# Attention with q/k normalisation and a two-matmul feed-forward on one core: unit loads ahead of the weight loads, LN transposes on the DMA queue, q and k transposes on TensorE up to unit 7, later unit loads on GpSimd's queue

## The chip, the cores and the metric

The kernel runs on one core of one Trainium2 chip. The metric is the device time of one execution in microseconds (us). Engines in the views: PE is TensorE (PEld its weight loads), DVE is VectorE, ACT is ScalarE, POOL is GpSimd, SP is SyncE, which does nothing here but issue DMAs.

## The reference

```python
q_n, k_n = rmsnorm(q, g_q), rmsnorm(k, g_k)          # q, k, v: (8, 12, 448, 64) float32
scores = (1/8) * q_n @ k_n^T                         # per batch and head, 448 x 448
attn = softmax(scores); x = attn @ v                 # heads side by side: (8, 448, 768)
xn = layernorm(x) * g_ln                             # over 768
out = x + relu(xn @ w_ch1) @ w_ch2                   # w_ch1 768 x 3072, w_ch2 3072 x 768
```

## The kernel before, in words

The work is staged by batch. While PE does the feed-forward of batch b, the attention of batch b+1 is cut into small steps that are put between the feed-forward's chunks of six matmuls. Only the attention of batch 0 stands alone, ahead of everything.

**Units and pairs.** A *unit* is what is loaded and prepared in one go: from batch 1 on, four heads, that is two *pairs* of heads. Batch 0 has units 0 to 3 (one, one, two and two pairs), batch 1 has units 4, 5 and 6, batch 2 has units 7, 8 and 9, and so on to unit 24. `load_unit` fills one tile `qkv` with k, q and v by nine DMAs (a main one and two small "left" ones each); the pool has two such tiles, so unit u+2 is loaded when unit u has been read for the last time.

**Preparation of a unit** (`pieces`, called by one-letter names). `a`, `c`: squares of k and q on ACT (L196). `d`, `e`: their sums on DVE (L199). `g` (`gq`, `gk`): reciprocal roots on ACT (L56, L57). `i`: k times the product of the two gains, `kg`, on POOL (L205; on DVE for the units of `DVE_KG`). `j`, `k`: k as a high and a low half in float16 (`khi` on ACT or POOL, L213 or L211; `klo` on DVE, L216). `l`, `m`: scaled q and its second copy (L63, L256). `v`, `w` (`z` both): v cast to float16 on POOL (L262, L268).

**Transposes of q and k.** Below unit `DMA_UNIT` PE transposes each pair (`trans_k`, L290 and L293; `trans_q`, L304 and L307), seven matmuls each through the one PSUM tile `tr`, and DVE copies it out (L295, L312). From `DMA_UNIT` on, SP issues DMA transposes of a whole unit instead: `x` (k: one large, two small, L235 and L238) and `y` (q: three and two, L245 and L248).

**Attention of a pair.** Seven score blocks (`scores`, L326, L329, L330), each followed by ACT's exponential (`E`, L332), and seven blocks of `values` (L355, L357); then DVE divides and writes `x` (L370 to L377).

**LN and feed-forward.** `stats`, `A`, `N` (L499, L514, L519) give the normalised tile `xn`; `X` (`ln_trans`) transposes it on PE (L546) and copies it to `xnT` (L551, or L549 on ACT). A batch has three tiles of 128 tokens, an odd batch a fourth one (`xl`), made of the leftovers of two batches. `up` makes `hT` (PE L564, ACT L566) and `down` the result (PE L577, DVE L581).

**What sets the order.** PE, ACT, POOL and SP run in the order in which the program emits; DVE's order is by a scheduler after the first attention. The first attention follows the written table `ORDER`, whose words are the names above with a unit or pair (`a5`), `S`/`V` with pair and block, `L5` a unit load, `W0` to `W2` thirds of the first weight, `W3`, `W4` halves of the second. Weights are loaded from POOL's queue, since the DMA casts them to float16. After that, `attention` makes a list of steps, seven to a pair (step 7p + i), and gives each unit's pieces their steps; `run_rest` spreads the steps over a batch's chunks so that they end `tail` chunks before the batch does. At that point it emits the LN of the next batch (`ln_list`).

Of the kernel before, what the change touches and what calls it, by code (L numbers as in the profile page):

```python
# [28 lines left out]
DVE_KG, POOL_HI, POOL_DUP, ACT_Q = (0, 1), (1, 2, 3, 4), (1, 2, 4, 5), (0, 1)  # L29
# [42 lines left out]
class _Fast:  # L72


    def __init__(self, ctx, tc, sh, q, k, v, g_ln, w1, w2, out):
        self.g_ln = g_ln
# [26 lines left out]
        self.rr = fix.tile([128, 2, 7 * B * NPAIR], FP32, name="rr_all", tag="rr_all")  # L103
# [23 lines left out]
    def load_first(self):  # L127
# [44 lines left out]
    def pieces(self, u):  # L172
# [9 lines left out]
        def begin():  # L182
# [4 lines left out]
            c["rf"] = self.rr[:, :, o:o + g]  # L187
# [16 lines left out]
        def kg():  # L204
            (nc.vector if u in DVE_KG else nc.gpsimd).tensor_tensor(  # L205
                out=c["t"][1], in0=c["t"][1],
                in1=sh.gprod.unsqueeze(1).broadcast_to([128, g, D]), op=ALU.mult)
# [77 lines left out]
    def trans_k(self, p):  # L285
# [3 lines left out]
        kT, ps = self.kU[0][:, 960 * (p % 2):960 * (p % 2) + 960], self.tr  # L289
# [7 lines left out]
    def trans_q(self, p):  # L297
# [5 lines left out]
        qT = self.qU[0][:, p % 2].rearrange("p e s -> p (e s)")  # L303
# [9 lines left out]
        kT = self.kU[0][:, 960 * (p % 2):960 * (p % 2) + 960]  # L313
        self.prs[p] = dict(q=qT, main=kT[:, 192:960], left=kT[:, 0:192])

    def scores(self, p, i):
# [6 lines left out]
        ps = self.ps_s.tile([128, 512], FP32, tag="psS", name="psS")  # L323
# [4 lines left out]
        else:  # L328
# [4 lines left out]
                             scale=self.rr[:, 1, g:g + 1], bias=EXP_BIAS)  # L333
# [53 lines left out]
    def first_attention(self):  # L387
# [7 lines left out]
        for x in ORDER:  # L395
# [28 lines left out]
    def attention(self):  # L424
# [445 lines left out]
```

## Time and profile before

| | |
|---|---|
| median of 3 runs | 649.29 us (648.17 to 650.2) |
| profiled execution | 649.09 us, of which the span of the trace is 647.3 us |
| DVE, ACT, POOL busy | 293.0, 362.7, 103.1 us |
| DMA issues | 160 DMA transposes, 21 unit loads of nine DMAs each |
| HBM read, written | 52.36 MB, 11.01 MB |

Four stages follow one another in the span: batch 0's attention, up to 66.4 us; batch 0's feed-forward beside batch 1's attention, up to 150.07 us; six batches of the same kind, up to 577.96 us; and the feed-forward of batch 7 alone. In a row of a timeline the first number is the start, the second the duration, and brackets tell how long the engine was idle before it and what ended that. In a row of waits stand the total, the count and the longest.

### The profile page before, as it was taken

How to read it: one execution, taken by the hardware profiler on the slowest of the kernel's cores; microseconds unless marked ns; L12 is line 12 of the kernel's file. 1: busy time of each engine (PE TensorE's matmuls, PEld its weight loads, DVE VectorE, ACT ScalarE, POOL GpSimd, SP SyncE). 2: the span in 40 equal slices, each digit the busy share in tenths (PEclk: the TensorE clock that was granted, in tenths of full speed). 3: DMA queues.
4: the chain of work that ended last, by engine and by line, in shares of the span. 5: the costliest groups of instructions: out<-in, count | busy, mean ns of one | idle time of the engine just before them, and what ended most of it. 6: DMA issues, size and time to landing. Idle time of an engine off the chain costs nothing.

```text
span 647.3 us, 11504 instructions
## 1 busy us (share of the span) xinstructions
PE 594.3 (92%) x4506; PEld 349.6 (54%) x4506; DVE 293.0 (45%) x633; ACT 362.7 (56%) x673; POOL 103.1 (16%) x116
## 2 busy tenths in 40 slices
PE   2873957999999999999999999999999999999995
PEld 1552534565556666665556666665556666654563
DVE  5795504573425625672434625582443621380011
ACT  5974736644874368635874288626874277314300
POOL 2942310220210202220220111210221100000000
PEclk9996879899999999999999999999999999999998
DMA  8999985554255354564255355455243230010011
GB/s 231 246 220 221 200 178 120 140 140 157 62 141 131 94 130 119 110 151 113 55 133 139 90 132 119 113 140 126 66 107 79 71 62 4 25 50 0 2 50 53
DMA packets 149836, 73.12 MB, mean 113 GB/s; under 512 B 99728, under 2 KB 144784, under 8 KB 149776
## 3 DMA queue, kind: packets, MB, share of 16 engines
q1 hardware_dynamic: 140960, 62.82, 39.4%
q0 software_dynamic: 8528, 9.44, 8.6%
q8 instruction: 37, 0.61, 0.4%
q14 instruction: 23, 0.19, 0.1%
q10 hardware_dynamic: 288, 0.07, 0.0%
HBM read 52.36 MB, written 11.01 MB: 98 GB/s over the span
## 4 chain that ended last, share of the span: by engine, by line
PE 74%; DVE 8%; SPq 7%; DMA 4%; ACT 3%; issue 2%; POOL 0%; ACTq 0%; DVEq 0%; POOLq 0%
PE psH L564 32%; PE psC L577 25%; PE psS L326 7%; PE oA L355 4%; SPq L125 4%; DVE xn L519 3%; DMA qkv<-in_v_dram 2%; PE oB L357 1%; SPq L245 1%; SPq L117 1%; DVE stat L499 1%; PE psX L546 1%; DVE khl L216 1%; ACT E L332 1%; PE psS L329 1%
## 5 line engine op out<-in xcount | busy, mean ns | idle before, releaser
L564 PE MATMUL psH<-xnT,w 128*128 128x512 f16 (+1 forms) x1152 | 250.4, 358 | 0.0
L332 ACT ACTIVATE E<-psS,rr_all 128x448 f16<-128x448 f32 x336 | 207.8, 632 | 71.1 <-PE psS L326 64.6
L577 PE MATMUL psC<-w,hT 128*128 128x384 f16 x1344 | 241.8, 326 | 1.6 <-DVE x L581 1.6
L566 ACT ACTIVATE hT<-psH 128x384 f16<-128x384 f32 (+1 forms) x192 | 105.0, 547 | 132.0 <-PE psH L564 130.8
L577 PEld LDWEIGHTS <-hT 128*128 128x128 f16 x1344 | 124.1, 98 | 72.7 <-issue 2.2
L564 PEld LDWEIGHTS <-w 128*128 128x128 f16 x1152 | 106.0, 99 | 85.1 <-issue 4.7
L326 PE MATMUL psS<-qU,kU 128*128 128x448 f16 x288 | 104.3, 365 | 17.7 <-DMA qU<-qn 10.5
L355 PEld LDWEIGHTS <-E 128*128 128x128 f16 x1008 | 71.6, 99 | 63.9 <-ACT E L332 11.8
L205 POOL TENSOR_TENSOR qkv<-qkv,gprod 128x896 f32<-128x896 f32 x21 | 43.7, 2082 | 325.6 <-issue 253.0
L355 PE MATMUL oA<-v,E 128*128 128x65 f16 x864 | 68.0, 196 | 5.6 <-ACT E L332 5.2
L581 DVE SCALAR_TENSOR_TENSOR x<-psC,rs_all,x 128x384 f32<-128x384 f32 x48 | 29.5, 617 | 85.7 <-PE psC L577 85.1
L199 DVE TENSOR_REDUCE ssq<-khl 128x14 f32<-128x896 f32 (+1 forms) x25 | 26.2, 1048 | 80.1 <-ACT khl L196 80.0
L370 DVE RECIPROCAL rec_all<-oA 128x6 f32<-128x6 f32 x48 | 9.3, 194 | 98.3 <-PE oA L355 98.1
L357 PE MATMUL oB<-v,E 128*128 128x65 f16 x288 | 52.6, 195 | 0.1
L326 PEld LDWEIGHTS <-kU 128*128 128x128 f16 x288 | 28.6, 100 | 36.5 <-issue 17.4
L63 DVE SCALAR_TENSOR_TENSOR qn<-qkv,rr_all 128x256 f16<-128x256 f32 (+2 forms) x81 | 26.9, 393 | 19.9 <-ACT rr_all L57 19.9
L199 DVE TENSOR_REDUCE ssq<-qn 128x14 f32<-128x896 f32 (+1 forms) x25 | 26.1, 1045 | 20.4 <-ACT qn L196 20.4
L357 PEld LDWEIGHTS <-E 128*128 128x128 f16 x336 | 33.0, 98 | 0.6 <-DVE xl L377 0.4
L216 DVE TENSOR_TENSOR khl<-qkv,khl 128x896 f16<-128x896 f32 x21 | 22.8, 1088 | 10.9 <-ACT khl L213 10.9
L372 DVE TENSOR_TENSOR x<-oA,rec_all 128x384 f32<-128x384 f32 x48 | 26.8, 558 | 1.5
L499 DVE BATCH_NORM_STATS2 stat<-x 128x6 f32<-128x256 f32 x72 | 26.1, 415 | 0.7
L262 POOL CAST v<-qkv 128x768 f16<-128x768 f32 x21 | 17.4, 828 | 35.6 <-PE oB L357 19.6
(87 smaller groups left out, 356.9 us busy)
## 6 DMA issues: line engine op xcount, KB each, us to landing
qkv<-in_k_dram SPq DMA_DIRECT2D x21, 384.0 KB, 3.4
qkv<-in_q_dram SPq DMA_DIRECT2D x21, 384.0 KB, 3.9
qkv<-in_v_dram SPq DMA_DIRECT2D x21, 384.0 KB, 4.2
out_dram<-x SPq DMA_DIRECT2D x20, 384.0 KB, 2.5
w<-in_moe_w_ch_dram POOLq DMA_DIRECT2D x3, 1536.0 KB, 20.3
w<-in_moe_w_ch_dram POOLq DMA_DIRECT2D x2, 2304.0 KB, 45.2
qU<-qn SPq DMA_TRANSPOSE x100, 2.4
out_dram<-x SPq DMA_DIRECT2D x8, 192.0 KB, 2.3
```

The lines of the kernel that those rows point to most:

```text
L199: nc.vector.tensor_reduce(out=c["ssq"][:, n], in_=c["sq", n], axis=AX.X, op=ALU.add)
L205: (nc.vector if u in DVE_KG else nc.gpsimd).tensor_tensor(out=c["t"][1], in0=c["t"][1], in1=sh.gprod.unsqueeze(1).broadcast_to([128, g, D] ...
L216: nc.vector.tensor_tensor(out=c["khl"][:, :, 1], in0=c["t"][1], in1=c["khl"][:, :, 0], op=ALU.subtract)
L326: nc.tensor.matmul(ps[:, 0:S], c["main"][:, ts(i, 128)], q[:, ts(h, S)], start=True, stop=True)
L332: nc.scalar.activation(out=c["E"][:, i], in_=ps[:, 0:S], func=AFT.Exp, scale=self.rr[:, 1, g:g + 1], bias=EXP_BIAS)
L355: nc.tensor.matmul(oA[:, t, cs], E[:, i, ts(t, 128)], rhs, start=(i == 0 and t == 0), stop=(i == 6 and t == 2))
L357: nc.tensor.matmul(oB[:, cs], E[:, i, 320:448], rhs, start=(i == 0), stop=(i == 6))
L499: nc.vector.bn_stats(out=self.st[b][:, t, 6 * s:6 * s + 6], in_=x[:, 256 * s:256 * s + 256])
L564: nc.tensor.matmul(ps[:, 0:N], sh.w1[:, dc, ts(f, 128)], xnT[:, dc, 0:N], start=(dc == 0), stop=(dc == NDC - 1))
L566: nc.scalar.activation(out=hT[:, f, 0:N], in_=ps[:, 0:N], func=AFT.Relu)
L577: nc.tensor.matmul(ps[:, 0:384], hT[:, f, ts(t, 128)], sh.w2[:, f, ts(g, 384)], start=(f == 0), stop=(f == NFF - 1))
L581: nc.vector.scalar_tensor_tensor(out=x[:, ts(g, 384)], in0=ps[:, 0:384], scalar=self.rs[:, b, t:t + 1], in1=x[:, ts(g, 384)], op0=ALU.mult ...
```

## The change

- First loads: k of pair 0 and its leftovers go out from ACT's queue beside q's on SP; the two gains follow on SP. Their product is made by DVE in unit 0's `kg`, and `gmax` at `G2`.
- `ORDER` is another table. The loads of units 4 and 5 (`L4 L5`) stand right behind `G`; `W0` stands behind `i3` (unit 3's `kg`), `W1` and `W2` further on, `W3` behind `m4`; `W4` is emitted with unit 6's first pieces.
- Units 5 to 7 get their q and k transposed on PE (`DMA_UNIT` 8), units 5 and 6 prepared at given steps (`EARLY`). The DMA transposes remain from unit 8 on.
- Unit loads are emitted one step later than before; from unit 9 on they go out from POOL's queue instead of SP's.
- From batch 1 on `ln_trans` is one DMA transpose per tile on SP, with no PSUM tile and no copy; the LN stands in one piece, `tail` is 13 chunks instead of 10, and `xn` has four buffers.
- From pair 15 on every third score block uses `tr`'s bank.
- Unit 2's `kg` moves from POOL to DVE, unit 5's copy of q from POOL to DVE; the reciprocal roots of q and k are two exponentials instead of one.

```diff
-DVE_KG, POOL_HI, POOL_DUP, ACT_Q = (0, 1), (1, 2, 3, 4), (1, 2, 4, 5), (0, 1)
+DVE_KG, POOL_HI, POOL_DUP, ACT_Q = (0, 1, 2), (1, 2, 3, 4), (1, 2, 4), (0, 1)
 ORDER = """
-b0 c0 e0 a0 gq0 d0 b1 i0 G j0 z0 a1 k0 c1 l0 i1 gk0 m0 d1 K0 Q0 e1 b2 g1 a2 l1 j1 d2 m1 S0.0
...
+b0 c0 e0 a0 d0 b1 i0 gq0 a1 G L4 L5 j0 z0 k0 gk0 l0 i1 m0 d1 c1 K0 Q0 e1 b2 j1 g1 a2 S0.0 S0.1
...
-DMA_UNIT = 5
+DMA_UNIT = 8
+PE_SET = (DMA_UNIT + 1) % 2
+EARLY = {5: (42, 49), 6: (48, 57)}
...
-        for n in range(2):
+        for n, eng in ((0, nc.sync), (1, nc.scalar)):
+            main(eng, n, 0)
+            left(eng, n)
+        for n in range(2):
-            main(nc.sync, n, 0)
-            left(nc.sync, n)
+            nc.sync.dma_start(self.sh.gg[:, n], self.gs[n].unsqueeze(0).broadcast_to([128, D]))
...
     def load_unit(self, u):
+        eng = self.nc.sync if u < 9 else self.nc.gpsimd
         for n in (1, 0, 2):
-            self.load_main(self.nc.sync, n, t[:, n, 0:6 * m], b, hs, 2 * m)
-            self.load_left(self.nc.sync, n, t[:, n, 6 * m:7 * m], b, hs, 2 * m)
+            self.load_main(eng, n, t[:, n, 0:6 * m], b, hs, 2 * m)
+            self.load_left(eng, n, t[:, n, 6 * m:7 * m], b, hs, 2 * m)
...
         def root(n=slice(0, 2)):
-            _rsqrt(nc, c["rf"][:, n], c["ssq"][:, n], c["rt"][:, n], D * 1e-6)
+            nc.scalar.activation(c["rt"][:, n], c["ssq"][:, n], AFT.Ln, bias=D * 1e-6)
+            for i in range(2)[n] if isinstance(n, slice) else (n,):
+                nc.scalar.activation(c["r", i], c["rt"][:, i], AFT.Exp, scale=-0.5)
...
-        ps = self.ps_s.tile([128, 512], FP32, tag="psS", name="psS")
+        if p > UNIT_PAIR[DMA_UNIT] and (7 * p + i) % 3 == 2:
+            ps = self.ps_tr.tile([128, 512], FP32, tag="tr", name="psS3")
+        else:
+            ps = self.ps_s.tile([128, 512], FP32, tag="psS", name="psS")
...
             e = max(7 * (p - 2) - 1, st + 5)
+            st, e = EARLY.get(u, (st, e))
             pieces = ["bai", "d", "c", "e", "j", "gv", "k", "l", "m", "w", "x", "y"]
             k = len(pieces) - 2
+            if u < DMA_UNIT:
+                pieces = pieces[:k]
             if u < nu - 2 and f"L{u + 2}" not in done:
-                todo.setdefault(e, []).append(lambda u=u: self.load_unit(u + 2))
+                todo.setdefault(e + 1, []).append(lambda u=u: self.load_unit(u + 2))
...
+                if u == 6 and x == 0 and "W4" not in done:
+                    todo[at].append(lambda: self.load_w2(1))
...
-        return [call("A", "N0", "N1", "N2", "R")] + [
-            call(f"X{t}", *([f"N{t + 3}"] if t + 3 < n else [])) for t in range(n)]
+        return [call("A", "N0", "N1", "X0", "N2", "X1", *(["N3"] if n > 3 else []), "X2",
+                     *(["X3"] if n > 3 else []), "R")]
...
             self.xnT = self.p_m.tile([128, NDC, 512], FP16, tag="xnT", name="xnT")
+        if b:
+            nc.sync.dma_start_transpose(self.xnT[:, :, ts(t, 128)], xn)
+            return
...
-        tail = 10
+        tail = 13
```

Line numbers of the changed kernel lie some 6 to 27 above those of the kernel before. On POOL's queue during the first attention, the weights stood in the kernel before as follows (`w_76` is the first weight, in thirds of 1024 columns; `w_66` the second, in halves of 384, whose room v's first load uses until the casts `v` and `vl` have read it; `L205` on `hT` is unit 3's `kg`, on `qkv` unit 4's). Two thirds of the first weight had gone out six rows further up, ahead of unit 2's `kg`.

```order
L205 TENSOR_TENSOR hT<-hT,gprod 128x896
L262 CAST v_116<-w_66 128x12x64
L268 CAST vl<-w_66 64x2x64 x2
L473 DMA w_76<-in_moe_w_ch_dram 128x6x1024
L211 CAST khl<-hT 128x14x64
L478 DMA w_66<-in_moe_w_ch_dram 128x24x384 x2
L205 TENSOR_TENSOR qkv<-qkv,gprod 128x896
```

In the changed kernel the queue reads from unit 3's `kg` to unit 4's:

```order
L215 TENSOR_TENSOR hT<-hT,gprod 128x896
L497 DMA w_71<-in_moe_w_ch_dram 128x6x1024
L272 CAST v_111<-w_66 128x12x64
L278 CAST vl<-w_66 64x2x64 x2
L221 CAST khl<-hT 128x14x64
L497 DMA w_71<-in_moe_w_ch_dram 128x6x1024 x2
L215 TENSOR_TENSOR qkv<-qkv,gprod 128x896
```

and further on, from unit 4's last v casts:

```order
L278 CAST vl<-qkv 64x2x64 x2
L266 COPY qn<-qn 128x14x64
L502 DMA w_66<-in_moe_w_ch_dram 128x24x384
L215 TENSOR_TENSOR qkv<-qkv,gprod 128x896 x2
L502 DMA w_66<-in_moe_w_ch_dram 128x24x384
```

The first third of the first weight has moved from ahead of unit 2's `kg` to behind unit 3's, and the halves of the second weight from ahead of unit 4's `kg` to behind unit 4's last piece and behind the `kg` of units 5 and 6.

On SP's queue, the end of the stretch in which batch 1's attention runs reads as follows in the kernel before: one unit's load, another unit's k and q transposes, then batch 0's first stores.

```order
L117 DMA qkv<-in_k_dram 128x4x192
L125 DMA qkv<-in_k_dram 64x2x64 x2
L117 DMA qkv<-in_q_dram 128x4x192
L125 DMA qkv<-in_q_dram 64x2x64 x2
L117 DMA qkv<-in_v_dram 128x4x192
L125 DMA qkv<-in_v_dram 64x2x64 x2
L235 DMA_TRANSPOSE kU_112<-khl 128x12x128
L238 DMA_TRANSPOSE kU_112<-khl 128x2x64 x2
L245 DMA_TRANSPOSE qU_114<-qn 128x4x128 x3
L248 DMA_TRANSPOSE qU_114<-qn 128x2x64 x2
L605 DMA out_dram<-x 128x384
L605 DMA out_dram<-x 128x768 x2
```

In the changed kernel the same place has the k and q transposes of unit 8, the first that go by DMA, and the four LN transposes of batch 1:

```order
L245 DMA_TRANSPOSE kU_107<-khl 128x12x128
L248 DMA_TRANSPOSE kU_107<-khl 128x2x64 x2
L255 DMA_TRANSPOSE qU_109<-qn 128x4x128 x3
L258 DMA_TRANSPOSE qU_109<-qn 128x2x64 x2
L569 DMA_TRANSPOSE xnT<-xn 128x6x128 x4
L632 DMA out_dram<-x 128x384
L632 DMA out_dram<-x 128x768 x2
```

The unit load has gone from the queue, and `xnT` stands between the unit's transposes and the stores.

The load now stands on POOL's queue. In the kernel before, two units' preparation reads there (the numbers tell buffers apart):

```order
L205 TENSOR_TENSOR qkv_674<-qkv_674,gprod_69 128x896
L262 CAST v16_116<-qkv_674 128x12x64
L268 CAST vl_117<-qkv_674 64x2x64 x2
L233 MEMSET kU0_112 128x2x64
L205 TENSOR_TENSOR qkv_937<-qkv_937,gprod_69 128x896
L262 CAST v16_116<-qkv_937 128x12x64
L268 CAST vl_117<-qkv_937 64x2x64 x2
```

In the changed kernel, from unit 7's `kg` on, with the load of unit 9 and then unit 8's `kg`:

```order
L215 TENSOR_TENSOR qkv_956<-qkv_956,gprod_67 128x896
L272 CAST v16_111<-qkv_956 128x12x64
L278 CAST vl_112<-qkv_956 64x2x64 x2
L119 DMA qkv_1314<-in_k_dram 128x4x192
L127 DMA qkv_1314<-in_k_dram 64x2x64 x2
L119 DMA qkv_1314<-in_q_dram 128x4x192
L127 DMA qkv_1314<-in_q_dram 64x2x64 x2
L119 DMA qkv_1314<-in_v_dram 128x4x192
L127 DMA qkv_1314<-in_v_dram 64x2x64 x2
L215 TENSOR_TENSOR qkv_1079<-qkv_1079,gprod_67 128x896
L272 CAST v16_111<-qkv_1079 128x12x64
```

Nine DMA instructions (six rows) now stand between one unit's last v cast and the next unit's `kg`.

More of the change, by code (lines that the diff above doesn't have):

```diff
@@ L72, with __init__ @@
 class _Fast:
-    def __init__(self, ctx, tc, sh, q, k, v, g_ln, w1, w2, out):
-        self.g_ln = g_ln
+    def __init__(self, ctx, tc, sh, q, k, v, gs, g_ln, w1, w2, out):
+        self.gs, self.g_ln = gs, g_ln
         self.tc, self.nc, self.sh = tc, tc.nc, sh
@@ L102, in __init__ @@
         nc.vector.memset(self.rec, 0.01)
-        self.rr = fix.tile([128, 2, 7 * B * NPAIR], FP32, name="rr_all", tag="rr_all")
+        self.rr = fix.tile([128, 7 * B * NPAIR], FP32, name="rr_all", tag="rr_all")
         self.rs = fix.tile([128, B, 4], FP32, name="rs_all", tag="rs_all")
@@ L186, in begin @@
             o = 7 * UNIT_PAIR[u]
-            c["rf"] = self.rr[:, :, o:o + g]
+            c["r", 0] = self.p_n.tile([128, 14], FP32, tag="rq", name="rq")[:, 0:g]
+            c["r", 1] = self.rr[:, o:o + g]
             c["qn"] = self.p_n.tile([128, 14, 2, D], FP16, tag="qn", name="qn")[:, 0:g]
@@ L404, in first_attention @@
                 nc.vector.tensor_scalar(out=gln, in0=gln, scalar1=XS, scalar2=None, op0=ALU.mult)
+                gmax = self.sh.gmax
+                nc.vector.tensor_reduce(out=gmax, in_=self.sh.gprod, axis=AX.X, op=ALU.max,
+                                        apply_absolute_value=True)
+                nc.vector.tensor_scalar(out=gmax, in0=gmax, scalar1=1.0 / K_MAX, scalar2=None,
+                                        op0=ALU.mult)
             elif key == "W":
@@ L440, in attention @@
                 at = st + (e - st) * x // (k - 1) if x < k else e + 1 + x - k
-                todo.setdefault(at, []).extend(self.prep_ops(u)[y] for y in names)
+                todo.setdefault(at, []).extend(
+                    self.prep_ops(u)[y] for y in names if f"{y}{u}" not in done)
+                if u == 6 and x == 0 and "W4" not in done:
+                    todo[at].append(lambda: self.load_w2(1))
         steps, mark = [], [0]
@@ L547, in ln_trans @@
                              start=(dc == 0), stop=(dc == NDC - 1))
-        if b == 0 and t < 2:
+        if t < 2:
             nc.scalar.copy(out=self.xnT[:, :, ts(t, 128)], in_=ps)
```

51 lines of the change are left out of this document (23 added, 28 removed).

## The prediction

> **What bounds the kernel now.** I read the busy time by stage first, to see where PE is not the bound. The columns are the stage, its length, then PE, PEld, DVE, ACT and POOL busy (with counts), the granted PE clock, the DMA share and GB/s.
>
> ```profile
> 0.00:47.60 47.60, 28.83 (x310) 18.21 (x310) 36.47 (x73) 35.66 (x68) 24.58 (x33) 1.00 1.02 233
> 47.60:66.40 18.80, 7.03 (x58) 3.98 (x59) 9.92 (x21) 9.06 (x16) 3.48 (x4) 0.63 1.24 221
> 66.40:150.07 83.67, 71.55 (x518) 42.67 (x516) 40.84 (x86) 45.95 (x88) 16.63 (x19) 0.90 0.74 156
> 150.07:577.96 427.89, 424.26 (x3287) 251.93 (x3286) 199.20 (x442) 257.73 (x478) 58.44 (x60) 1.00 0.41 100
> 577.96:647.30 69.34, 62.66 (x338) 32.77 (x337) 6.58 (x15) 14.33 (x24) 0.00 (x0) 0.97 0.08 27
> ```
>
> From 150 us on PE is busy 99% at full clock: only less PE work helps there. Before that no compute engine is full: from 47.6 to 66.4 us PE works 7.03 of 18.80 us at a clock of 0.63, while the DMA engines are full. So I looked at who waits there (ACT, then POOL, then SP).
>
> ```profile
> 50.25 0.95 ACT L196 ACTIVATE khl<-qkv 128x896 f32<-128x896 f32 x1 [5.31 <-DMA qkv<-in_k_dram]
> 62.57 0.95 ACT L213 ACTIVATE khl<-qkv 128x896 f16<-128x896 f32 x1 [5.42 <-POOL qkv L205]
> 58.59 0.88 POOL L262 CAST v<-qkv 128x768 f16<-128x768 f32 x1 [12.96 <-DMA qkv<-in_v_dram]
> 60.47 2.07 POOL L205 TENSOR_TENSOR qkv<-qkv,gprod 128x896 f32<-128x896 f32 x1
> 24.77 1.47 SPq L117 DMA_DIRECT2D qkv<-in_k_dram  x1
> 16.36 1.82 POOL L473 DMA_DIRECT2D w<-in_moe_w_ch_dram  x2
> ```
>
> All of it is unit 5. Its k, issued at 24.77 us, holds ACT until 50.25; its v holds POOL, in whose queue `kg` stands behind the v cast, and `kg` holds ACT again until 62.57. Its load crawls because the first weight went out at 16.36, ahead of it. The answers on DMA, for 15 to 20 us (weights hardly begun), 24.7 to 33.7 us and 49.5 to 54.2 us, show the price; the last number of an issue is us to landing, q0 is the weights' queue:
>
> ```profile
> DMA packets 2029, 1.69 MB, mean 339 GB/s; under 512 B 280, under 2 KB 1889, under 8 KB 2029
> ...
> DMA packets 1534, 1.97 MB, mean 219 GB/s; under 512 B 320, under 2 KB 783, under 8 KB 1533
> q0 software_dynamic: 766, 1.54, 89.8%
> qkv<-in_k_dram SPq DMA_DIRECT2D x1, 384.0 KB, 23.6
> ...
> qkv<-in_k_dram SPq DMA_DIRECT2D x1, 384.0 KB, 14.4
> ```
>
> Beside the weights a unit's load gets 1.97 - 1.54 = 0.43 MB in 9 us, 48 GB/s instead of 339.
>
> In the third stage PE is idle for 83.67 - 71.55 = 12.1 us; a row of its waits (total, times, longest) and two rows of its timeline tell why and what follows:
>
> ```profile
> PE psS L326 <- DMA qU<-qn: 10.5, 2, 6.5
> 88.32 2.12 PE L564 MATMUL psH<-xnT,w 128*128 128x384 f16 x6
> 93.79 1.14 PE L564 MATMUL psH<-xnT,w 128*128 128x384 f16 x6
> ```
>
> The q transposes by DMA are late twice, 10.5 of the 12.1 us, and after such idling the clock is half: the same six matmuls take 2.12 instead of 1.14 us.
>
> **The change part by part**, against the span of 647.3 us.
>
> ```profile
> 3.40 1.27 SPq L125 DMA_DIRECT2D hT<-in_k_dram  x2
> L57 ACT ACTIVATE rr_all<-rt 128x28 f32<-128x28 f32 (+2 forms) x26 | 5.8, 225 | 0.8
> ```
>
> *Lead-in.* Units 4 and 5 are issued when only first loads are in flight: 2 x 1.376 MB (three times four heads of 448 x 64 float32) at 339 GB/s is 8 us, so they land some 8 us behind the first loads, before ACT asks for them, and both its waits go: -5.3 -5.4. That ACT sets the pace is seen from its 35.66 us busy in 47.6. k of pair 0 goes out beside q instead of behind it, with two issues of 0.64 us for its leftovers alone; between 0 and about 2 us I take -1.0. Against it stand four more exponentials of the roots on ACT, 0.225 each (+0.9). Unit 2's `kg` on DVE (36.47 of 47.6 busy) is hidden, at worst 1.2. Sum -10.8: the first feed-forward matmul at 55.6 instead of 66.4.
>
> ```profile
> 27.36 0.22 PE L290 MATMUL tr<-id,khl 128*128 128x128 f16 x1
> 27.42 0.50 PE L293 MATMUL tr<-id,khl 128*128 128x128 f16 x6
> 27.75 0.84 PE L326 MATMUL psS<-qU,kU 128*128 128x448 f16 x2
> L295 DVE COPY kU<-tr 128x960 f16<-128x960 f16 x8 | 5.2, 656 | 2.3 <-PE tr L293 2.2
> 43.29 1.08 DVE L63 SCALAR_TENSOR_TENSOR qn<-qkv,rr_all 128x896 f16<-128x896 f32 x1
> ```
>
> *Batch 0's feed-forward.* The DMA transposes of units 5 to 7 go: -10.5 of waits, and about four half-clock groups behind the two stalls, at 2.12 - 1.14 = 0.98 each, with the score blocks between them: -4.4. PE transposes six pairs more. A pair's K takes 27.75 - 27.36 = 0.39 us of PE, Q the same, so +6 x 0.78 = +4.7; the DVE copies (12 x 0.65 = 7.8 us) lie under DVE's 40.84 of 83.67.
>
> New wait: unit 6's load needs unit 4's tile, last read by DVE at 44.4 us (the row of L63, `l4`), and then meets the weights, now 12 us later. Its k is due behind four `up` groups and one pair's transposes, 55.6 + 4 x 0.97 + 0.78 = 60.3. With the landing times above it comes at 44.4 + 14.4 = 58.7 (no wait) to 44.4 + 23.6 = 68.0 (7.7 of wait). ACT waits with relus and exponentials behind it, and PE follows within three PSUM tiles. I take 63.3, since the weight pieces in flight are of both kinds: +3.0, and +0.5 for q; unit 7 costs 0 to 4 in the same way, taken 0. The weights land at most the 12 us later that they start later. Of the idle 12.1 us above 10.5 are `qU`, so PE did not wait for weights before; the last half is now needed three quarters through a stretch of some 74 us, at 55.6 + 56 = 111 us: hidden, and a wait there is rival 4.
>
> *LN transposes.* 25 tiles (4 in batches 1, 3, 5, 7, 3 in 2, 4, 6) leave PE.
>
> ```profile
> 217.25 6.99 PE L577 MATMUL psC<-w,hT 128*128 128x384 f16 x42
> 219.60 1.08 DVE L499 BATCH_NORM_STATS2 stat<-x 128x6 f32<-128x256 f32 x3
> 220.93 2.81 DVE L519 SCALAR_TENSOR_TENSOR xn<-x,stat,gln 128x768 f16<-128x768 f32 x3
> 225.75 0.50 PE L546 MATMUL psX<-id,xn 128*128 128x128 f16 x6
> 226.08 1.14 PE L577 MATMUL psC<-w,hT 128*128 128x384 f16 x6
> 228.37 0.81 PE L564 MATMUL psH<-xnT,w 128*128 128x384 f16 x4
> L546 PE MATMUL psX<-id,xn 128*128 128x128 f16 x168 | 13.9, 219 | 2.9 <-DVE x L581 1.8 <-DVE xn L519 1.1
> ```
>
> One tile is 226.08 - 225.75 = 0.33 us: -25 x 0.33 = -8.3, and -1.8 for PE's waits on DVE that are listed beside it. A new feed-forward needs the whole `xnT`. Here the last values end at 217.25 and `xn` is done at 223.74, 6.5 us later; a fourth tile adds a third of either row, 0.36 + 0.94, about 1.4 with its aggregate. A DMA transpose of a tile is not in this trace; the nearest are:
>
> ```profile
> kU<-khl SPq DMA_TRANSPOSE x60, 2.8
> 161.03 1.52 SPq L235 DMA_TRANSPOSE kU<-khl  x1
> 169.52 2.51 SPq L248 DMA_TRANSPOSE qU<-qn  x2
> ```
>
> So the last tile is there 6.5 + 1.4 + 2.8 = 10.7 us after the last values, and 13 chunks of six at 0.97 (42 took 6.99 with the last one's drain) are 12.6: hidden, with 1.9 us to spare. Ahead in SP's queue stand a unit's transposes, 172.03 - 161.03 = 11 us from the first to the last row, emitted seven steps before the end; a step is (427.89/6 - 12.6)/42 = 1.4 us, so they clear about 1.2 us after the last values, before the first `xn` at 4.6. Cost 0; at worst each boundary stays 2 us late, +14.
>
> *Unit loads on POOL.* 16 units (9 to 24), each with nine DMA instructions ahead of the next unit's `kg`.
>
> ```profile
> L473 POOL DMA_DIRECT2D w<-in_moe_w_ch_dram x3 | 2.7, 904 | 0.0
> L478 POOL DMA_DIRECT2D w<-in_moe_w_ch_dram x2 | 2.8, 1410 | 0.0
> 22.37 1.66 POOL L256 COPY qn<-qn 128x896 f16<-128x896 f16 x1 [1.08 <-PE psS L326]
> 67.80 0.93 POOL L256 COPY qn<-qn 128x896 f16<-128x896 f16 x1 [5.26 <-DVE rec_all L370]
> ```
>
> These loads have fewer pieces than L473's, so I take 0.9 us: 9 x 0.9 + 2.07 = 10.2 us until `kg` is done, while ACT's `khi` comes six steps, 8.4 us, after the load: ACT waits 1.8 us. Behind that stand exponentials and relus, which PE bridges with two or three score tiles and three others, a step each: cost 0, at most 16 x 1.8 = +29. SP in turn loses nine issues ahead of each unit's transposes, which nobody waited for.
>
> The Trainium skill's page "SBUF — State Buffer" (section "SBUF: two separate sides") warns against this part: a DMA issued from GpSimd has its descriptors written by GpSimd, and certain VectorE operations lock it out of SBUF until they end. The pair of copies above agrees that POOL is held up, 1.66 against 0.93 us, but no row here shows a DMA instruction so held. By that rule each of the nine could wait for a VectorE instruction, and the sum would come out as the third rival's; by the rows of L473 and L478 it stays at 621.
>
> *Sum.* 647.3 - 10.8 - 10.5 - 4.4 + 4.7 + 3.5 - 8.3 - 1.8 = 619.7 us of span; with the 1.8 us that lie around it in the profiled execution (649.09 us, 0.2 under the median) 621.5, so 621.
>
> **Rivals.**
> 1. *The load wait moves to unit 6 and 7.* For: the landing of 23.6 us. Against: the second half of the weights is issued only behind unit 6's `kg`. With 7.7 + 0.5 + 4 instead of 3.5 us: 630.
> 2. *The LN transposes end the wait at each batch.* For: SP runs in order, and unit loads now share the DMA engines with them instead of standing ahead in one queue. Against: the 1.9 us spare. At +2 us in seven places: 635.
> 3. *Slower: POOL's queue becomes the bound.* If each DMA instruction is stretched as the copy is, by 0.73 us, `kg` comes 9 x 0.73 = 6.6 us later still, ACT waits 8.4 and PE, after some 3 us of cover, 5.4 in each of 16 units: 621 + 86 = 707. The change turns into a loss from 28/16 = 1.75 us of PE stall per unit on. Against: the five weight issues at 0.9 and 1.41 ran while DVE was busiest.
> 4. *Hidden anyway.* The first 84 us move the same bytes, so PE might only wait elsewhere, for weights. The lead-in and the clock are then not won back, only the 10.5, 8.3 and 1.8 less 4.7: 633 or so. Against: the first third of the first weight is alone in its need at 56 us.
>
> **How the numbers follow.** Forecast 0.58, rival 1 0.16, rival 2 0.11, rival 3 0.07, rival 4 0.08. The forecast's own bounds are 621 - 3.5 - 4 (clock drops and waits that I left in) = 613 and 629; rivals 1, 2 and 4 fill 629 to 635. 611 to 636 leaves out rival 3 and about a tenth besides. A measurement of this kernel tells 0.3% (2 us) from no change. Slower gets rival 3's 0.07, no change 0.03, faster the rest.
>
> **What would show it.** Right: no ACT wait on `in_k_dram` or on `kg` before the first `psH`, which starts at 53 to 58 us; batch 1's first 512-column `psH` at 125 to 134 us; no psS wait on `qU`; later batches 1.0 to 1.6 us shorter each. Wrong: PE idle before the first `psH` of a batch, ended by DMA `xnT`; ACT waiting for POOL's `kg` in every unit, with PE idle beside it; DMA instructions on POOL well over 0.9 us.

## The result, and the profile after

The changed kernel took 633.12 us (median of 4 runs, 631.58 to 634.16) against 648.91 beside it: a ratio of 0.9753, interval 0.9726 to 0.9779. It is 15.8 us faster; I had forecast 28. The profiled execution took 631.58 us, the lowest of the four, with a span of 629.8. One run of experiment 7 took 899.9 us at a granted clock of 0.66, as one run of the kernel before did, and both are left out of the numbers below.

By stage (columns as before: stage, length, PE, PEld, DVE, ACT, POOL busy, clock, DMA share, GB/s):

```profile
0.00:47.60 47.60, 27.77 (x303) 17.60 (x303) 35.75 (x69) 36.79 (x74) 20.43 (x32) 1.00 0.97 227
47.60:61.61 14.01, 7.88 (x65) 5.37 (x66) 11.67 (x25) 8.23 (x17) 3.55 (x3) 0.64 1.18 219
61.61:144.67 83.06, 71.40 (x575) 44.65 (x576) 45.72 (x85) 46.44 (x90) 28.86 (x38) 0.96 0.75 152
144.67:560.40 415.73, 415.49 (x3162) 245.19 (x3160) 189.81 (x425) 256.47 (x494) 139.79 (x187) 1.00 0.55 113
560.40:629.80 69.40, 62.67 (x339) 32.78 (x337) 5.71 (x10) 14.33 (x24) 0.00 (x0) 0.99 0.08 27
```

| stage | before | forecast | changed | with both repairs (last experiment) |
|---|---|---|---|---|
| lead-in, to the first feed-forward matmul | 66.4 | 55.6 | 61.6 | 63.9 |
| batch 0's feed-forward | 83.7 | 75.7 | 83.1 | 71.1 |
| six batches | 427.9 | 419.2 | 415.7 | 415.7 |
| last feed-forward | 69.3 | 69.3 | 69.4 | 69.4 |
| span | 647.3 | 619.7 | 629.8 | 620.1 |

The forecast column is its own terms put into their stages (the LN's four tiles of batch 1 in the second). The other columns are one profile each; how far the lead-in varies between executions is told in the last section. The lead-in gave 4.8 of 10.8 us, the six batches gave 12.2 of 8.7, and batch 0's feed-forward gave 0.6 of 8.0. There PE is still idle for 83.06 - 71.40 = 11.7 us, as before, but for other reasons. The timeline shows the first:

```profile
67.97 2.09 POOL L215 TENSOR_TENSOR qkv<-qkv,gprod 128x896 f32<-128x896 f32 x1 [16.80 <-ACT khl L202]
70.00 1.47 POOL L502 DMA_DIRECT2D w<-in_moe_w_ch_dram  x1
71.47 0.66 POOL L278 CAST vl<-qkv 64x128 f16<-64x128 f32 x2
...
72.16 0.37 SPq L119 DMA_DIRECT2D qkv<-in_k_dram  x1
...
83.25 0.95 ACT L202 ACTIVATE khl<-qkv 128x896 f32<-128x896 f32 x1 [4.38 <-DMA qkv<-in_k_dram]
88.17 0.95 ACT L202 ACTIVATE qn<-qkv 128x896 f32<-128x896 f32 x1 [2.55 <-DMA qkv<-in_q_dram]
...
84.77 0.35 PE L339 MATMUL psS<-qU,kU 128*128 128x448 f16 x1 [4.45 <-ACT E L345]
```

The square of unit 7's k waits for its load. The load goes out at 72.16, 0.03 us after POOL's two `vl` casts (71.47 + 0.66), which are unit 5's and the last reads of the tile. They stand in POOL's queue behind unit 6's `kg` and the last weight half, `kg` behind unit 6's square. PE stops behind ACT's exponentials, 4.45 us at 84.77.

The second, 40 us on:

```profile
111.87 1.55 SPq L245 DMA_TRANSPOSE kU<-khl  x1
...
120.45 2.90 SPq L258 DMA_TRANSPOSE qU<-qn  x2
...
122.34 0.95 ACT L202 ACTIVATE khl<-qkv 128x896 f32<-128x896 f32 x1 [3.10 <-DMA kU<-khl]
128.19 0.95 ACT L202 ACTIVATE qn<-qkv 128x896 f32<-128x896 f32 x1 [3.85 <-DMA qU<-qn]
...
123.87 0.35 PE L339 MATMUL psS<-qU,kU 128*128 128x448 f16 x1 [2.09 <-ACT E L345]
129.72 0.35 PE L342 MATMUL psS<-qU,kU 128*128 128x448 f16 x1 [2.85 <-ACT E L345]
```

ACT does not wait for data, since unit 9's own load, issued from 95.77 us on, had landed by 105: it wants to *write*. The squares of unit 9 are put as scratch into the `khl` and `qn` buffers, which unit 8's DMA transposes, just issued, still read. Units below 8 have no such transposes any more, and in the six batches ACT waits for no transpose, so this meets unit 8 alone.

The LN boundary, which I had called hidden, is:

```profile
134.80 5.20 SPq L569 DMA_TRANSPOSE xnT<-xn  x4
...
139.79 5.04 PE L604 MATMUL psC<-w,hT 128*128 128x384 f16 x30
144.67 1.46 PE L591 MATMUL psH<-xnT,w 128*128 128x512 f16 x6
```

PE goes from the last `psC` into the new batch without a gap, and in the six batches it is busy for 415.49 of 415.73 us. The nine DMA instructions of a unit load on POOL cost less than I had taken, 3 x 0.79 + 6 x 0.605 = 6.0 us instead of 8.1 (groups: count, busy, mean ns):

```profile
L127 POOL DMA_DIRECT2D qkv<-in_k_dram x32 | 19.2, 605 | 0.0
L119 POOL DMA_DIRECT2D qkv<-in_v_dram x16 | 12.7, 791 | 0.0
```

### The profile page after: what moved, and what is told of

Its sections match the earlier page's. It is cut to its first block, busy times and chain, and to the rows that moved or that the text cites. A ratio compares the mean times of both kernels' runs of the same rounds, so it can differ in the third digit from the quotient of the medians.

```text
span 629.8 us, 11369 instructions
## 1 busy us (share of the span) xinstructions
PE 585.2 (93%) x4440; PEld 345.6 (55%) x4440; DVE 288.6 (46%) x613; ACT 362.3 (58%) x697; POOL 192.6 (31%) x258
## 4 chain that ended last, share of the span: by engine, by line
PE 82%; DMA 5%; DVE 4%; issue 3%; SPq 1%; ACT 1%; POOL 0%; DVEq 0%; ACTq 0%; POOLq 0%
PE psC L604 34%; PE psH L591 32%; PE psS L339 7%; PE oA L368 5%; DMA qkv<-in_q_dram 2%; DMA qkv<-in_k_dram 2%; PE oB L370 2%; PE psS L342 1%; PE psS L343 1%; DMA qU<-qn 1%; DVE ssq L205 1%; DVE khl L226 1%; DVE qn L65 1%; ACT E L345 1%; DVE x L385 1%
## 5 line engine op out<-in xcount | busy, mean ns | idle before, releaser
L591 PE MATMUL psH<-xnT,w 128*128 128x512 f16 (+1 forms) x1152 | 246.8, 354 | 0.3 <-DVE rec_all L383 0.3
L604 PE MATMUL psC<-w,hT 128*128 128x384 f16 x1344 | 236.0, 327 | 0.0
L604 PEld LDWEIGHTS <-hT 128*128 128x128 f16 x1344 | 126.7, 98 | 76.7 <-issue 1.5
L591 PEld LDWEIGHTS <-w 128*128 128x128 f16 x1152 | 104.6, 98 | 82.9 <-issue 2.2
L339 PE MATMUL psS<-qU,kU 128*128 128x448 f16 x288 | 101.8, 360 | 14.9 <-ACT E L345 12.8
L119 POOL DMA_DIRECT2D qkv<-in_k_dram x16 | 12.8, 801 | 140.7 <-ACT E L345 76.2
L205 DVE TENSOR_REDUCE ssq<-khl 128x14 f32<-128x896 f32 (+1 forms) x25 | 26.2, 1046 | 53.0 <-ACT khl L202 52.9
L205 DVE TENSOR_REDUCE ssq<-qn 128x14 f32<-128x896 f32 (+1 forms) x25 | 26.2, 1047 | 35.0 <-ACT qn L202 34.9
L65 DVE SCALAR_TENSOR_TENSOR qn<-qkv,rq 128x256 f16<-128x256 f32 (+1 forms) x72 | 26.4, 424 | 17.9 <-ACT rq L210 17.9
## 6 DMA issues: line engine op xcount, KB each, us to landing
w<-in_moe_w_ch_dram POOLq DMA_DIRECT2D x3, 1536.0 KB, 15.8
```

Source lines behind the costliest of these rows:

```text
L65: nc.vector.scalar_tensor_tensor(out=out, in0=x, scalar=8.0, in1=r.unsqueeze(2).broadcast_to([x.shape[0], g, D]), op0=ALU.mult, op1=ALU.mult)
L205: nc.vector.tensor_reduce(out=c["ssq"][:, n], in_=c["sq", n], axis=AX.X, op=ALU.add)
L339: nc.tensor.matmul(ps[:, 0:S], c["main"][:, ts(i, 128)], q[:, ts(h, S)], start=True, stop=True)
L591: nc.tensor.matmul(ps[:, 0:N], sh.w1[:, dc, ts(f, 128)], xnT[:, dc, 0:N], start=(dc == 0), stop=(dc == NDC - 1))
L604: nc.tensor.matmul(ps[:, 0:384], hT[:, f, ts(t, 128)], sh.w2[:, f, ts(g, 384)], start=(f == 0), stop=(f == NFF - 1))
```

## The experiments

Differences are against the changed kernel's 633.12 us. The kernel before, timed beside each group, had medians of 649.4 to 650.0 us; a difference of a microsecond is not to be read.

**1. Unit 5's leftover v cast earlier.**

```diff
-S5.6 a5 i5 V5.3 V5.4
+S5.6 a5 i5 w5 V5.3 V5.4
```

> The changed kernel with one move: unit 5's cast of its leftover v (vl, two instructions on POOL) stands right behind unit 5's kg instead of behind unit 6's kg and the last weight half. Theory (queue order): in the changed kernel these casts are the last readers of the tile that unit 7's load needs; they end at 72.13, and the load goes out at 72.16. Moved, the last reader is DVE's klo of unit 5, which ended at 66.67: unit 7's k goes out some 5.4 us earlier, ahead of the last weight half (issued at 70.0), lands at 77 to 78, ACT's waits on in_k (4.38) and in_q (2.55) and PE's idle behind them go, and the time falls by 5 to 7 us against the changed kernel. Rival (bandwidth): the load crawls beside the weights however early it is issued, k still lands at 82 or later, ACT still waits over 3 us, and the time falls by less than 2 us.

627.51 us (625.45 to 629.87), ratio 0.9663 (0.9639 to 0.9687): 5.6 less. In its timeline the casts and the load:

```profile
53.90 0.64 POOL L278 CAST vl<-qkv 64x128 f16<-64x128 f32 x2
...
70.50 0.37 SPq L119 DMA_DIRECT2D qkv<-in_k_dram  x1
...
82.83 0.95 ACT L202 ACTIVATE khl<-qkv 128x896 f32<-128x896 f32 x1 [0.21 <-PE tr L303]
```

The load goes out 5.6 us after this run's first feed-forward matmul (64.94) instead of 10.6, ahead of the last weight half (issued at 74.18 here), and unit 7's square no longer waits for it. That the order in the queues is the cause is shown. The rival falls: issued ahead of the weight half, k lands 7.5 us after its issue instead of 9.6, and q 6.9 instead of 12.3.

**2. Unit 9's preparation three steps later.**

```diff
-EARLY = {5: (42, 49), 6: (48, 57)}
+EARLY = {5: (42, 49), 6: (48, 57), 9: (89, 97)}
```

> The changed kernel with unit 9's squares (and the rest of its preparation) starting three steps later (step 89 instead of 86). Theory (a buffer still being read): ACT's waits of 3.10 us on the DMA transposes of kU and 3.85 us on those of qU at 122 to 128 us are unit 9's squares, written as scratch into the khl and qn buffers which unit 8's DMA transposes, issued at 111.87 to 123.35, are still reading; three steps later, about 5 us, the first wait is gone and the second is under 1.5, PE's idle there (2.09 and 2.85 us) shrinks, and the time falls by 3 to 5 us against the changed kernel. Rival (the transposes are late for their own scores): the idle moves to PE's score blocks of unit 8, a psS wait on DMA kU or qU appears, and the time stays within 1 us.

626.95 us (626.06 to 627.42), ratio 0.9652 (0.9634 to 0.9669): 6.2 less, above the upper end of 5. All of PE's waits in batch 0's feed-forward (total, times, longest):

```profile
PE psS L339 <- ACT E L345: 5.1, 2, 4.6
PE psS L342 <- ACT E L345: 0.8, 2, 0.6
PE psH L591 <- DVE rec_all L383: 0.4, 1, 0.4
```

What is left is unit 7's stall (4.6). No score block waits for a transpose, so the rival falls. ACT's wait on qU did not shrink as I had expected (5.1 us instead of 3.85). It now lies behind all but one of the batch's exponentials, up to 132.39 us, while PE runs 55 matmuls of `psC` in a row from 127.16 on, so it no longer matters.

**3. LN transposes back on PE** (with the LN in pieces and `tail` 10).

```diff
-        if b:
-            nc.sync.dma_start_transpose(self.xnT[:, :, ts(t, 128)], xn)
-            return
...
-        tail = 13
+        tail = 10
```

> The changed kernel with the LN transposes of batches 1 to 7 back on PE (six matmuls and a DVE copy per tile, the LN in pieces, tail 10), all else as changed. By the forecast's term it should be 10.1 us slower than the changed kernel (25 tiles of 0.33 and 1.8 of waits). By what the stage of the six batches showed, 12.2 us shorter in the changed kernel, of which at most 0.7 us can be the third score bank, it should be 12 to 15 us slower: 21 tiles at some 0.55 us each, the drain and refill of the matmul pipe around each group included, and four more tiles in batch 1.

647.32 us (645.66 to 650.62, 12 runs), ratio 0.9975 (0.9960 to 0.9991): 14.2 more. Its six batches take 427.34 us against 415.73, that is 11.6 / 21 = 0.55 us a tile, and nearly the 427.89 of the kernel before: the gain there is the LN's. Of the 11.6 us PE idles for 2.9, where I had 1.8, and is busy for 8.7, where 21 tiles at my 0.33, from one start to the next, give 6.9. What the other 1.8 us of work are stays open. The four tiles of batch 1 add 1.4 us, so the stages show 13.0; the lead-in, in which the two programs are the same, differs by 1.4 us between the two profiles.

**4. q and k of units 5 to 7 by DMA again.**

```diff
-DMA_UNIT = 8
+DMA_UNIT = 5
```

> The changed kernel with q and k of units 5 to 7 transposed by DMA again, as before the change (DMA_UNIT 5), loads and weights in the new order. Forecast's steps: waits of PE on qU of 10.5 us and half-clock groups of 4.4 come back and 4.7 us of PE transposes go: 10 us slower than the changed kernel. Rival: it was the late loads that made those transposes late, and with the loads ahead of the weights the waits on qU would have gone without moving the transposes to PE: then 2 to 5 us faster than the changed kernel, with no wait of a score block on qU over 1 us.

643.28 us (641.44 to 644.18), ratio 0.9909 (0.9893 to 0.9925): 10.2 more, the forecast's 10.5 + 4.4 - 4.7. Two rows of waits of PE and two of SP's timeline:

```profile
PE psS L339 <- DMA qU<-qn: 24.2, 1, 24.2
PE psS L342 <- ACT E L345: 1.0, 1, 1.0
```
```profile
73.80 0.37 SPq L119 DMA_DIRECT2D qkv<-in_k_dram  x1
...
84.43 8.10 SPq L245 DMA_TRANSPOSE kU<-khl  x1
```

With the loads ahead the transposes come later than before, not earlier: they stand in SP's queue behind unit 7's load, which itself crawls beside the weights. The rival is wrong. But the size agrees with my terms partly by chance, since one wait of 24.2 us takes the place of two that made 10.5, while the stalls of units 7 and 9 are absent.

**5. First loads as before.**

```diff
-        for n, eng in ((0, nc.sync), (1, nc.scalar)):
-            main(eng, n, 0)
-            left(eng, n)
         for n in range(2):
-            nc.sync.dma_start(self.sh.gg[:, n], ...)
+            nc.scalar.dma_start(self.sh.gg[:, n], ...)
+        for n in range(2):
+            main(nc.sync, n, 0)
+            left(nc.sync, n)
```

> The changed kernel with only the first loads as before the change: the two gains first, from ACT's queue; k of pair 0 and its leftovers behind q on SP. The profiles of the last four kernels (which have the changed first loads) showed what the first profile of the changed kernel did not: the gain g_k landed 7.1 us after its issue (3.4 there), DVE waited 2.1 to 2.5 us for it at 10.8 us, ACT 2.7 to 3.1 us for k of pair 1 at 11.3 us, and the first feed-forward matmul came at 63.0 to 64.9 us instead of 61.6. Theory (order of the first loads): with the gains first, the product is there at 5 us as in the kernel before, DVE has no such wait, and the first feed-forward matmul comes at 61 to 62.5 us: 1 to 3 us faster than the changed kernel. The forecast's own term for this step says the reverse: 1.0 us slower. Rival (all DMA stops for some 2 us near 8 to 11 us on this chip, whatever is in flight): ACT or DVE still waits 2 us for a first load near 11 us, and the time stays within 1 us.

633.57 us (631.70 to 635.05), ratio 0.9754 (0.9734 to 0.9774): no difference that can be read, so my theory's gain is not there, and the forecast's loss of 1.0 us can't be told from nothing. DVE no longer waits for the gain, but q and k come later: the first square of k is at 9.51 us instead of 7.29 in the second experiment, and the product is made at 10.66, hardly sooner. The product's row in the second experiment's timeline, and the squares of q and k in this kernel's:

```profile
10.83 0.23 DVE L214 TENSOR_TENSOR gprod<-w 128x64 f32<-128x64 f32 x1 [2.26 <-DMA w<-in_g_k_dram]
```
```profile
7.40 0.58 ACT L202 ACTIVATE qn<-hT 128x448 f32<-128x448 f32 x1 [4.20 <-DMA hT<-in_q_dram]
9.51 0.58 ACT L202 ACTIVATE khl<-hT 128x448 f32<-128x448 f32 x1 [1.54 <-DMA hT<-in_k_dram]
```

**6. All unit loads on SP.**

```diff
-        eng = self.nc.sync if u < 9 else self.nc.gpsimd
+        eng = self.nc.sync if u < 99 else self.nc.gpsimd
```

> The changed kernel with the unit loads 9 to 24 on SP's queue, as before the change, instead of POOL's. Forecast: moving them cost 0 (nobody waited for SP's issues, and POOL has room), so the time stays within 1.5 us of the changed kernel. Rival: they must not stand in SP's queue ahead of the LN transposes and the units' transposes; a load that waits for its tile then holds the transposes behind it, PE idles before the first psH of a batch on DMA xnT or in score blocks on DMA qU, and the time is 5 to 20 us longer.

640.60 us (639.89 to 642.16), ratio 0.9868 (0.9851 to 0.9886): 7.5 more. All of PE's waits in the six batches, and the worst place:

```profile
PE psH L591 <- DMA xnT<-xn: 8.9, 3, 5.0
```
```profile
429.68 2.72 PE L591 MATMUL psH<-xnT,w 128*128 128x512 f16 x6 [5.03 <-DMA xnT<-xn]
```

The six batches take 427.20 us, 11.5 more, and the matmuls behind such a stall run at about half speed (2.72 instead of 1.46 us). Before this place a unit's load holds SP's queue from 404.34 to 409.99 us, that unit's transposes follow up to 422.28, and the LN's go out at 423.01. The second rival of the prediction is real, and what keeps it away is the move of the loads to POOL, which I had priced at nothing. (Batch 0's feed-forward is 4.6 us shorter: unit 9's square meets no transposes there.)

**7. Loads of units 4 and 5 behind the weights again.**

```diff
-... gq0 a1 G L4 L5 j0 ... S0.3 d2 K1 e2 S0.4 V0.0 ... i3 W0 d3 ... j3 W1 k3 W2
+... gq0 a1 G j0 ... S0.3 L4 W0 L5 d2 K1 e2 S0.4 W1 V0.0 ... i3 d3 ... j3 k3 W2
```

> The changed kernel with the loads of units 4 and 5 again behind the first two thirds of the first weight, as before the change (L4 W0 L5 ... W1 behind pair 0's scores), all else as changed. Forecast's step: 5.3 and 5.4 us of ACT's waits on unit 5's k and kg come back, 10.7 us slower than the changed kernel, first feed-forward matmul at 72 to 75 us. Theory (DVE paces the lead-in, and the waits that went had mostly been covered): 3 to 5 us slower, first feed-forward matmul at 65 to 69 us.

646.45 us (645.67 to 648.46, 7 runs), ratio 0.9961 (0.9945 to 0.9976): 13.3 more, above either expectation. The first feed-forward matmul is at 76.02. Rows of waits of ACT and of POOL:

```profile
ACT E L345 <- PE psS L343: 12.3, 1, 12.3
```
```profile
POOL v L272 <- DMA qkv<-in_v_dram: 15.5, 1, 15.5
```

In the changed kernel a cast of unit 5's v stands ahead of unit 4's `khi` on POOL. Where the load is late, POOL stands there until 55.03 and everything with it. So this undoes more than the kernel before had.

**8 and 10. More work in the lead-in, on DVE and on ACT.**

```diff
-S0.3 d2 K1 e2 S0.4 ... d3 S1.6 V1.1 e3 V1.2
+S0.3 d2 d2 K1 e2 e2 S0.4 ... d3 d3 S1.6 V1.1 e3 e3 V1.2
```
```diff
-a2 S0.0 ... c2 S0.3 ... a3 z2 ... c3 S1.3
+a2 a2 S0.0 ... c2 c2 S0.3 ... a3 a3 z2 ... c3 c3 S1.3
```

> The changed kernel with four more instructions on DVE in the lead-in: the sums of squares of units 2 and 3 (d2, e2, d3, e3, 1.09 us each) are made twice, same result, 4.4 us of DVE's time between about 20 and 33 us. Theory (DVE paces the lead-in): the first feed-forward matmul is 3 to 4.4 us later and the time 3 to 4.4 us longer than the changed kernel's. Rival (ACT paces it, as the forecast took it, or the DMA): at most 1.5 us longer.

641.19 us (638.94 to 642.39), ratio 0.9876 (0.9858 to 0.9894): 8.1 more for 4.4 us of DVE.

> The changed kernel with four more instructions on ACT in the lead-in: the squares of units 2 and 3 (0.94 us each) are made twice, same result, 3.8 us of ACT's time between about 17 and 28 us. Theory (DVE alone paces the lead-in): at most 1.5 us longer than the changed kernel. Rival (ACT paces it, as the forecast took it): 3 to 4 us longer. A third reading: both are full and hand each other work, so that any extra there lengthens the lead-in by at least its own time, 4 us or more.

637.62 us (637.13 to 640.27), ratio 0.9814 (0.9793 to 0.9835): 4.5 more for 3.8 us of ACT. The first feed-forward matmuls, on DVE's kernel and on ACT's:

```profile
71.34 1.24 PE L591 MATMUL psH<-xnT,w 128*128 128x384 f16 x6 [0.31 <-DVE rec_all L383]
```
```profile
68.81 1.68 PE L591 MATMUL psH<-xnT,w 128*128 128x384 f16 x6 [0.31 <-DVE rec_all L383]
```

The first feed-forward matmul came between 61.6 and 64.5 us where nothing was added. Both additions lengthen the lead-in by at least their own time, DVE's by about twice as much: the third reading. That DVE alone paces the lead-in is refuted, since ACT's 3.8 us could then have cost 1.5 at most.

**9. Less work on DVE.**

```diff
-DVE_KG, POOL_HI, POOL_DUP, ACT_Q = (0, 1, 2), (1, 2, 3, 4), (1, 2, 4), (0, 1)
+DVE_KG, POOL_HI, POOL_DUP, ACT_Q, POOL_LO = (0, 1), (1, 2, 3, 4), (1, 2, 4), (0, 1), (3,)
...
-            nc.vector.tensor_tensor(out=c["khl"][:, :, 1], ...
+            (nc.gpsimd if u in POOL_LO else nc.vector).tensor_tensor(out=c["khl"][:, :, 1], ...
```

> The changed kernel with two instructions of the lead-in taken from DVE and given to POOL: unit 2's kg (as it was before the change; 1.08 us on DVE) and unit 3's low half of k (1.09 us), the latter ahead of the second third of the first weight in POOL's queue. Theory (DVE paces the lead-in): 2.2 us of DVE go, and since 4.4 us more made it 7.9 us longer, the first feed-forward matmul comes 2 to 4 us earlier, at 59 to 61.5 us, and the time falls by 2 to 4 us against the changed kernel. Rival (DVE is on the path only where ACT hands it late work, so that less of it gains nothing): within 1 us, or slower by up to 2 us, since each takes 2.1 us on POOL.

634.41 us (631.21 to 635.60), ratio 0.9745 (0.9723 to 0.9767): no gain, as the rival said. The two instructions take 2.45 and 1.88 us on POOL, but no engine waits for POOL there by more than 1.2 us. DVE waits where the instruction was, for ACT's root of q:

```profile
23.90 1.09 DVE L65 SCALAR_TENSOR_TENSOR qn<-hT,rq 128x896 f16<-128x896 f32 x1 [1.37 <-ACT rq L210]
```

**11. The new order of loads and weights alone, in the kernel before.**

```diff
-G j0 ... S0.3 L4 W0 L5 K1 ... S0.4 W1 V0.0 ... i3 d3 ... Q3 W2 V1.5
+G L4 L5 j0 ... S0.3 K1 ... S0.4 V0.0 ... i3 W0 d3 ... Q3 W1 W2 V1.5
```

> The kernel before the change with one part alone: the loads of units 4 and 5 right behind the gain of the LN in SP's queue, the first third of the first weight behind unit 3's kg, the second beside the third. Everything else (transposes, LN, unit loads, DMA of q and k from unit 5) as before. Forecast's step: ACT's two waits on unit 5 go, first feed-forward matmul at 55.6 to 56 us instead of 66.43, 10 us faster than the kernel before if the later weights cost nothing. Theory (DVE's backlog stood hidden under those waits): first feed-forward matmul at 59 to 63 us, 3 to 8 us faster.

647.55 us (647.27 to 648.99), ratio 0.9958 (0.9945 to 0.9972): 2.4 less than the 649.98 beside it. The first feed-forward matmul, and the largest of PE's waits behind it:

```profile
60.88 1.14 PE L564 MATMUL psH<-xnT,w 128*128 128x384 f16 x6
```
```profile
PE psS L326 <- DMA qU<-qn: 19.6, 2, 18.1
```

The lead-in is 5.5 us shorter, not 10.7. And 5.2 go back in batch 0's feed-forward (88.9 us instead of 83.7), where the transposes of q now land 13.0 us after their issue (median of five) instead of 4.5, beside the weights that go out later: 19.6 us of waiting instead of 10.5. (The profile is the slowest of the five runs, so its two stages add up to less than the 2.4.) Alone the load order brings 2.4 us; the rest of it pays only together with the transposes on PE.

This lead-in, of 60.88 us, is shorter than that of every profile of the changed kernel's own start (61.61 to 64.49), though q's first square came late, at 7.61 us against 6.79 in the changed kernel's profile. So the rest of the change lengthens the lead-in. Which part of it does was not tried.

**12. Both repairs** (the edits of 1 and 2).

> The changed kernel with both moves of the first two experiments: unit 5's leftover v cast right behind unit 5's kg, and unit 9's preparation three steps later. Theory (the two stalls lie at different places, 79 to 88 us and 122 to 130 us, and each was lost whole): the gains add, 633.1 - 5.6 - 6.2 = 621.3 us, between 619.5 and 623; PE has no wait over 1.5 us between the first feed-forward matmul and the end. Rival (the same slack is won twice): 625 us or more, with a wait of ACT of over 3 us on a load or a transpose that again stops PE.

620.30 us (619.25 to 622.04), ratio 0.9553 (0.9534 to 0.9571): 12.8 less, and faster than both kernels; the gains, 5.6 and 6.2, add. Its second stage, and all of PE's waits from 61.5 to 550 us:

```profile
63.90:135.02 71.12, 69.52 (x574) 44.11 (x575) 44.44 (x84) 45.83 (x89) 28.23 (x36) 0.97 0.88 177
```
```profile
PE psS L342 <- ACT E L345: 0.8, 2, 0.6
PE psS L339 <- ACT E L345: 0.5, 2, 0.3
PE psH L591 <- DVE rec_all L383: 0.4, 1, 0.4
PE psX L573 <- DVE xn L543: 0.3, 1, 0.3
PE tr L314 <- DVE kU L305: 0.3, 1, 0.3
```

PE is idle for 1.6 of 71.12 us.

## Why the prediction was right, and where it was not

Faster, and inside 611 to 636, with 12 us between the forecast and the median. But 633.12 lies above the forecast's own bounds of 613 to 629, where only its rivals were to come, and at the very 633 of rival 4, whose mechanism did not happen. That it fell inside the range is luck in part: two waits worth 5.6 and 6.2 us (1, 2), where the sum had 3.5, and a lead-in that gave less than half of its term met a gain of the LN larger than its own term. Step by step:

- **Lead-in, -10.8: mis-sized, -4.8.** Both waits of ACT on unit 5 went, as said. The step that failed is "That ACT sets the pace is seen from its 35.66 us busy in 47.6": from it I took every microsecond of those waits as one of the lead-in, though the same row had DVE busy for 36.47. The rows for 14 to 53 us, before and changed, show two engines nearly equal (the numbers behind the length are PE, PEld, DVE, ACT, POOL busy):

```profile
14.00:53.00 39.00, 27.82 (x302) 17.34 (x301) 30.60 (x56) 31.21 (x57) 23.36 (x27) 0.95 1.13 239
```
```profile
14.00:53.00 39.00, 27.95 (x304) 17.21 (x303) 33.43 (x61) 33.29 (x64) 23.27 (x27) 0.98 1.03 233
```

  DVE and ACT are each busy for some 33 of 39 us and hand each other sums, roots and copies in a fixed order. More on either costs at least itself (8, 10), less on DVE gains nothing (9), and the new order alone brings 5.5 (11). While ACT stood still before, DVE worked off its queue. The rows of ACT's two waits in the kernel before:

```profile
44.94:50.25 5.31, 1.38 (x24) 0.99 (x20) 3.42 (x9) 0.00 (x0) 0.69 (x1) 0.88 1.18 217
57.15:62.57 5.42, 1.80 (x15) 0.80 (x14) 3.19 (x4) 0.00 (x0) 3.48 (x4) 0.69 1.25 220
```

  DVE is busy for 3.42 and 3.19 us of them, 6.6 of 10.7, and idle for 4.1, which is near the 4.8 that were won. That the 6.6 us were worth nothing is argued from these rows and from 8 to 11, not shown by a run of its own. The -1.0 for k on ACT's queue can't be told from nothing (5), and the 1.2 that `kg` on DVE might cost at worst gives no gain when it is taken away (9).
- **Waits on qU, clock and PE transposes, -10.5 -4.4 +4.7: right in sum.** With the two stalls gone the stage is 71.1 us, where these terms and the LN's four tiles give 72.2. Putting the transposes back costs 10.2 (4), a weaker sign, since the waits there are others.
- **New wait, +3.5 at unit 6: wrong unit.** Unit 6's squares did not wait; unit 7, "0 to 4, taken 0", cost 5.6 (1). I had followed the landing times, but not what frees the tile: two small casts behind a weight's issue in POOL's queue. This is rival 1, at its later unit and larger there.
- **Not in the sum: 6.2 us at unit 9** (2). I asked of the DMA transposes that remained only whether they come in time for their scores, not who next writes the buffers that they read.
- **LN transposes, -10.1: right in kind, 13.0 by the stages and 14.2 by the medians of (3).** The boundary cost of 0 was right, rival 2 stayed away, and later batches are 12.2 / 6 = 2.0 us shorter each, above my 1.0 to 1.6. Batch 1's first 512-column `psH` came at 144.67 us, not at 125 to 134; with the repairs at 135.02.
- **POOL loads, 0: right as a cost, wrong as a value.** No `kg` was late: the DMA instructions, at 0.60 to 0.82 us each, stayed under the 0.9 I had taken, and rival 3 stayed away. The LN term rests on this part: without it 7.5 us are lost (6).
- **Rival 4** did not come as it was told: no row of PE's waits names a weight. Its other half, that the lead-in's wait is hidden anyway, came true for a part, under work of DVE.

Against the forecast's span the stages stand at +6.0, +7.4, -3.5 and +0.1 us, together 10.1 with rounding. That the repaired kernel meets the forecast's 621 within a microsecond is chance to a degree: its lead-in is 8.3 us longer than forecast, the next two stages 4.6 and 3.5 shorter.

## What to carry to other kernels

A wait that goes is worth its length only if no other engine was working off a backlog under it. Look at what the other engines did during the wait, and try which of them sets the time by adding work to each. When a transfer is late, look for the last reader of the buffer that it fills, in every queue, not only at bandwidth; and when a copy becomes a DMA, look for who next writes its *source*. Parts of a change can be worth little alone and much together (4, 6 and 11 each lose what another part won).

## What I had not expected of the hardware

The start is not as repeatable as the rest. With the same program up to that point, the first feed-forward matmul came at 61.61, 63.01, 63.73 and 64.49 us (the changed kernel and experiments 3, 6 and 2), while the six batches took 415.73 or 415.74 us in the changed kernel and in experiments 7 to 10 and 12 alike. In the late ones the gain g_k landed 7.0 to 7.1 us after its issue instead of 3.4, and SP's issues stood for 2 to 3 us near 9 us. All ten profiles of other kernels with these first loads are late in this way (6.7 to 7.3 us), so the changed kernel's own profile is the exception. With the old first loads the kernel before has an early start (q's first square at 5.89 us), but in experiments 5 and 11 q came late too, at 7.40 and 7.61 us. What holds the DMA engines there stays open. So the 4.8 us won in the lead-in compare an early profile with an early one; the latest of the four would give 1.9 against the same profile of the kernel before.

DMA instructions of unit loads on POOL took 0.60 to 0.64 us (small ones) and 0.78 to 0.82 us (main ones), all 144 of them, while DVE was busy 46% of the span. The Trainium skill's page "SBUF — State Buffer" (section "SBUF: two separate sides") warns that VectorE can lock out GpSimd as it writes descriptors; no DMA instruction of these loads shows such a hold, and moving them to this queue gained 7.5 us in this kernel. But the loads do land later than from SP's queue in experiment 6: in the six batches v's main part needs 7.4 us from issue to landing (median) instead of 4.3, and q's 5.2 instead of 3.9. Whether that is such a hold or the transposes, which now run beside the loads instead of behind them, the runs do not tell.
